# Attention and gated FFN on one core: when the first weights, the second quarters' scores, the output weights and batch 1's turns are issued

## The chip, the cores and the metric

One core of a Trainium2 chip runs the whole kernel. The time of a run is the device time in microseconds (us) of that core. The engines are TensorE (PE in the profile; PEld is its weight load), VectorE (DVE), ScalarE (ACT), GpSimd (POOL) and SyncE (SP, which here only issues DMAs). Each has its own queue of instructions and works through it in order; an instruction that waits holds up all that stand behind it on its engine. DMAs are issued from two queues: SyncE's (q1 in the profile) and GpSimd's (q0).

## The reference: what is computed

Attention over 8 batches of 8 heads, 576 positions, head size 64, with 16 beacon keys and values in front that every query sees; then a feed-forward network over the 4,608 rows that result.

```
k_all, v_all = concat(beacon_k, k), concat(beacon_v, v)      # 592 keys
scores = q @ k_all.T / sqrt(D)                               # causal, except for the beacons
a = softmax(scores)
x = (a @ v_all) with the heads side by side                  # 4608 x 512
out = (relu(x @ w_gate) * (x @ w_val)) @ w_out               # d_ff 1536
```

Inputs and output are float32; the kernel computes in bf16 with float32 sums.

## The kernel before, in words

**Attention.** Scores are made transposed, keys on the partitions and queries along the row, so exp's result is at once the moving operand of the product with v. A *unit* (L319) is one slot of up to 1,024 scores per partition: `qk` (L329) writes it into one of two double-bank PSUM buffers (`s_ps`), `exp` (L340) is one ScalarE instruction over it, and where the causal diagonal crosses it GpSimd sets the upper part to zero (the mask, L351). A part of a unit is named (g, ci, kt): g is the half of the heads (0 for heads 0 to 3, 1 for heads 4 to 7), ci the chunk of queries (240, 256 and 80 of them), kt the tile of 128 keys. When all parts of a chunk are through exp, the next step runs `av` (L363; its matmuls stand at L379): the product with v and, with a column of ones, the row sums. Then VectorE takes the reciprocal of the sums (`invert`, L387) and scales into xT (`scale`, L392). `note` (L396) keeps the least and greatest reciprocal in two VectorE operations, for a test at the end of the program whether a general path is needed; it has no other use.

**FFN.** A tile of 512 rows of x gives twelve `up` groups (four matmuls with wg at L413, ReLU on ScalarE at L416, four matmuls with wv at L422, the product hT on VectorE at L424) and then four `down` groups (twelve matmuls with wo at L429, a ScalarE copy at L432, a store). The products of `up` lie in two FFN banks (`f_ps`), or the second of them in an `s_ps` buffer where `spare` is set.

**The order of work.** The program is written out step by step in one Python loop over `plan` (L463), and each engine keeps that order. Batch 0 has steps 0 to 6, two units a step. Steps 7 to 10 have no attention, only FFN work of batch 0: no group, three, three, two. Batch 1 has steps 11 to 17 with one FFN group each; from step 18 on, seven steps a batch with FFN groups by a credit of time. `s2` in the code is 11, batch 1's first step. Within a step the order is: the `qk` of both units (with `between[s]` after the first), exp of the first unit, `av` and `invert` of the chunks that are due, the first half of the planned loads and casts, the FFN groups with exp of the second unit and `scale` among them, the rest of the planned actions, and then `later_half[s]`, what `after(s, ...)` registered.

**How data comes in.** Batches 0 and 1 bring q and k in *quarters*: 256 positions (i = 0 or 1) of four heads (g), cast to bf16 and turned on TensorE by eight transposes (L282), then moved from PSUM into qT or kT (L283). Batch 0's quarters are loaded by SyncE and cast by an engine (`cast_first`), batch 1's are loaded and cast by GpSimd's DMA (`load_second`, L271). Their last 64 positions (*tails*) and the beacon keys are turned by `turn_rows` (L300). Later batches bring tiles of 128 rows by SyncE, three loads a step, cast them on GpSimd a step later (L245, L249) and turn q and k with a DMA transpose another step later (L254); `fetch` (L584) registers this, and batch 2's starts in step 10. Batch 1's five value tiles are loaded by SyncE after a one-element memset on GpSimd (L227) lets the first go; casts of the values stand on GpSimd.

**The weights.** `load_w` (L309) issues two casting DMAs from GpSimd for a range of columns of wg or wv, `load_wo` (L315) one for half of wo. Before the change: columns 0 to 383 of both in `after(0)`, behind the casts of batch 0's first two value tiles; the rest of wg in `after(1)`, of wv in `after(2)`; wo in `after(7)`, behind batch 1's quarter loads.

The diff touches the order of the units (L140), the helpers from L498 to L520, the registrations up to L582 and the loop from L621 to L665.

Of the kernel before, what the change touches and what calls it, by code (L numbers as in the profile page):

```python
# [16 lines left out]
def general_path(tc, q, k, v, beacon_k, beacon_v, out, ident, wg, wv, wo):  # L17
# [123 lines left out]
    ((0, 0, 0),), ((0, 0, 1), (1, 0, 1)), ((1, 0, 0),), ((0, 1, 3), (1, 1, 3)),  # L141
    ((0, 1, 2),), ((0, 1, 1),), ((0, 1, 0),), ((1, 1, 2),), ((1, 1, 1),), ((1, 1, 0),),
# [11 lines left out]
def kernel(  # L154
# [15 lines left out]
    P = 128  # L170
# [298 lines left out]
    with tc.manual_schedule():  # L469
# [25 lines left out]
        def f_quarter():  # L495
            return f_ps.tile([P, 2, 2, P], BF16, name="f")

        def turn_first(i, g):  # L498
            first.turn_quarter("k", i, g, f_quarter(), dve)()
            first.turn_quarter("q", i, g, f_quarter(), act if i == 0 and g == 0 else dve)()  # L500

        def cast_first(i, g):
            first.cast_quarter("k", i, g, dve)
            first.cast_quarter("q", i, g, act if i == 0 else dve)
# [5 lines left out]
        def load_both(n0, n1):  # L510
            load_w(wg, moe_w_gate, n0, n1)
            load_w(wv, moe_w_val, n0, n1)

        def turn_two(x, i):
            for n in "kq":
                ps = s_ps.tile([P, 2, NP, 2, P], BF16, name="s")
                for move in [x.turn_quarter(n, i, g, ps[:, g, :2], (dve, act)[g])
                             for g in range(2)]:
                    move()
# [8 lines left out]
        later_half, between = {}, {}  # L528

        def after(step, action):  # L530
            later_half.setdefault(step, []).append(action)
# [5 lines left out]
        def turn_second_half():  # L537
            for g in range(2):
                turn_first(1, g)

        between[0] = lambda: turn_first(0, 1)
        after(0, lambda: cast_first(1, 0))
# [3 lines left out]
        after(0, lambda: load_both(0, 384))  # L546
        between[1] = turn_second_half
# [6 lines left out]
        after(3, lambda: turn_tails(first))  # L554
# [10 lines left out]
        after(7, lambda: load_wo(0, 6))  # L565
        after(7, lambda: load_wo(6, 12))
        for t in range(NKT):
            after(s2 - 1 + t // 2, lambda t=t: second.cast("v", t, pool))

# [10 lines left out]
        after(s2 - 1, lambda: turn_two(second, 0))  # L580
        after(s2, lambda: turn_two(second, 1))
# [25 lines left out]
        for s, (b, i, quota) in enumerate(plan):  # L607
# [14 lines left out]
            for j, u in enumerate(units):  # L622
                u.qk()
                if j == 0 and s in between:
                    between[s]()
            if units:
                units[0].exp()
            chunks, due = due, []
# [17 lines left out]
            for j, (kind, _, run) in enumerate(mine):  # L646
                if j == 0 and other and (kind == "down" or len(mine) == 1):
                    other.pop().exp()
                ups = kinds.count("up")
                run(b is None or (ups > 1 and j == (1 if ups > 2 else 0)))  # L650
                if j == 0:
                    for c in chunks:
                        c.scale()
                        notes.append(c.note)
                if other:
                    other.pop().exp()
            if not mine:
                for c in chunks:
                    c.scale()
                    notes.append(c.note)  # L660
                if other:
                    other.pop().exp()
            for act_ in acts + later_half.pop(s, []):
                act_()
            while len(notes) > (6 if s < 8 else 3 if s == 8 else 0):  # L665
                notes.pop(0)()
# [8 lines left out]
        run_sp()  # L675
        for t0, _ in spans:
            queue += ffn_tiles[t0 // M_TILE].groups(0, M_TILE, 0, M_TILE // P)
# [42 lines left out]
```

## Time and profile before

| | us |
|---|---|
| five runs | 398.41, 399.14, 398.06, 397.07, 399.34 |
| their median | 398.41 |
| the profiled execution, its own time | 399.94 |
| its span, first to last instruction | 398.2 |
| TensorE busy | 371.7 (93%) |
| VectorE, ScalarE, GpSimd busy | 207.3, 191.2, 121.3 |
| first `up` matmul, first `down` matmul | 32.88, 72.85 |
| mean granted TensorE clock | 0.992 |
| moved by DMA | 49.84 MB |

A group line of the profile names the line of the kernel, the engine, the operation, the tile written and the one read, the count, and the busy time with the mean of one instruction in ns; behind the last bar stands the idle time of that engine just before, and what ended it. In the timeline the first number is the start from the span's first instruction, the second the length. In the chain of work that ended last, each line is a piece of time and who held the work up in it. A table of stretches gives busy us of each engine between two moments, the granted TensorE clock as a share of full speed, the busy share of the DMA engines and what they moved. The DMA view counts packets, bytes and time for each queue.

### The profile page before, as it was taken

The numbers are of one execution on the slowest core, as the hardware profiler recorded it, in microseconds if no ns is written. First come the engines' busy times: TensorE is split into PE (matmuls) and PEld (weight loads), VectorE is DVE, ScalarE is ACT, GpSimd is POOL, SyncE is SP. The second block draws the span as 40 slices with busy tenths as digits, with TensorE's granted clock in tenths as the row PEclk, the third lists the DMA queues.
The fourth block names the chain that finished last, engine by engine and source line by source line (L and its number), as shares of the span: only waits on it lengthen the run. The fifth ranks groups of instructions, "written<-read, shape, count | busy, mean of one in ns | idle before, by whom it ended". The sixth has DMA issues, their size and how long they took to land.

```text
span 398.2 us, 10157 instructions
## 1 busy us (share of the span) xinstructions
PE 371.7 (93%) x4265; PEld 187.2 (47%) x4265; DVE 207.3 (52%) x336; ACT 191.2 (48%) x264; POOL 121.3 (30%) x213
## 2 busy tenths in 40 slices
PE   3778858999999999999999999999999999999994
PEld 2454433554554455545454545444544454444441
DVE  3766727736663666455646574557455643512420
ACT  3562264556463655465546455645455633323321
POOL 1858039424342335233524351435111100000000
PEclk9999998999999999999999999999999999999998
DMA  7999997949934882488348933985200011011002
GB/s 214 203 207 191 175 239 164 180 141 213 184 80 128 204 181 61 134 203 186 74 113 197 207 78 101 208 194 92 96 28 2 2 57 50 2 48 59 2 28 85
DMA packets 145555, 49.84 MB, mean 125 GB/s; under 512 B 133216, under 2 KB 139872, under 8 KB 145504
## 3 DMA queue, kind: packets, MB, share of 16 engines
q1 hardware_dynamic: 137536, 43.37, 46.4%
q0 software_dynamic: 7968, 5.77, 9.8%
q8 instruction: 35, 0.57, 0.6%
q14 instruction: 16, 0.13, 0.1%
HBM read 38.27 MB, written 9.44 MB: 120 GB/s over the span
## 4 chain that ended last, share of the span: by engine, by line
PE 88%; DVE 5%; DMA 2%; POOL 2%; issue 1%; ACT 1%; SPq 0%; DVEq 0%; POOLq 0%; ACTq 0%
PE f L413 24%; PE f L429 24%; PE s L422 12%; PE f L422 11%; PE ab L379 7%; PE s L335 6%; PE os L379 3%; DVE r L387 2%; DMA wide<-in_q_dram 1%; DVE hT L424 1%; DMA raw<-in_v_dram 1%; DVE xT L392 1%; POOL e L351 1%; DVE least L399 0%; POOL v L245 0%
## 5 line engine op out<-in xcount | busy, mean ns | idle before, releaser
L343 ACT ACTIVATE e<-s 128x1024 bf16<-128x1024 f32 (+2 forms) x112 | 105.0, 962 | 29.8 <-PE s L335 29.2
L413 PE MATMUL f<-xT,wg 128*128 128x512 bf16 x432 | 112.0, 382 | 0.8 <-DVE r L387 0.8
L416 ACT ACTIVATE g<-f 128x512 f32<-128x512 f32 x108 | 64.6, 598 | 88.9 <-PE f L413 84.7
L351 POOL TENSOR_SCALAR_AFFINE_SELECT e<-e 128x512 bf16<-128x512 bf16 (+2 forms) x80 | 46.5, 592 | 169.5 <-ACT e L343 158.8
L429 PE MATMUL f<-wo,hT 128*128 128x512 bf16 x432 | 97.3, 379 | 0.0
L387 DVE RECIPROCAL r<-os 128x240 f32<-128x240 f32 (+2 forms) x45 | 61.0, 1355 | 55.4 <-PE os L379 54.8
L424 DVE TENSOR_TENSOR hT<-g,s 128x512 bf16<-128x512 f32 x56 | 38.4, 687 | 60.5 <-PE s L422 59.5
L422 PEld LDWEIGHTS <-wv 128*128 128x128 bf16 x432 | 42.4, 98 | 53.0 <-issue 3.0
L429 PEld LDWEIGHTS <-hT 128*128 128x128 bf16 x432 | 41.0, 98 | 48.5
L424 DVE TENSOR_TENSOR hT<-g,f 128x512 bf16<-128x512 f32 x52 | 35.7, 687 | 51.4 <-PE f L422 50.7
L413 PEld LDWEIGHTS <-wg 128*128 128x128 bf16 x432 | 39.4, 98 | 46.6 <-issue 1.5
L422 PE MATMUL s<-xT,wv 128*128 128x512 bf16 x224 | 57.5, 379 | 0.3 <-DVE hT L424 0.3
L432 ACT COPY ob<-f 128x512 f32<-128x512 f32 x36 | 21.1, 586 | 74.2 <-PE f L429 54.9
L422 PE MATMUL f<-xT,wv 128*128 128x512 bf16 x208 | 54.2, 384 | 0.3 <-DVE hT L424 0.3
L379 PE MATMUL ab<-e,v 128*32 128x80 bf16 (+4 forms) x1320 | 40.2, 236 | 5.1 <-POOL e L351 3.1
L249 POOL CAST half<-raw 128x512 bf16<-128x512 f32 (+2 forms) x60 | 36.4, 624 | 15.3 <-DMA raw<-in_k_dram 6.3
L335 PE MATMUL s<-qT,kT 64*128 64x80 bf16 (+3 forms) x704 | 36.3, 237 | 4.0 <-DVE qT L283 1.7
L335 PEld LDWEIGHTS <-kT 64*128 64x128 bf16 x704 | 21.4, 98 | 27.4 <-issue 25.0
L379 PEld LDWEIGHTS <-v 128*32 128x32 bf16 (+1 forms) x1408 | 27.2, 99 | 14.0 <-issue 8.2
L379 PE MATMUL os<-e,ones 128*32 128x240 bf16 (+4 forms) x660 | 32.6, 234 | 0.0
L245 POOL CAST v<-raw 128x512 bf16<-128x512 f32 (+1 forms) x40 | 25.9, 653 | 14.1 <-DMA raw<-in_v_dram 14.1
L392 DVE TENSOR_TENSOR xT<-ab,r 128x480 bf16<-128x480 f32 (+2 forms) x45 | 24.9, 553 | 0.7
(47 smaller groups left out, 123.0 us busy)
## 6 DMA issues: line engine op xcount, KB each, us to landing
out_dram<-ob SPq DMA_DIRECT2D x36, 256.0 KB, 2.1
raw<-in_v_dram SPq DMA_DIRECT2D x24, 256.0 KB, 4.8
raw<-in_q_dram SPq DMA_DIRECT2D x24, 256.0 KB, 4.1
raw<-in_k_dram SPq DMA_DIRECT2D x18, 256.0 KB, 3.7
raw<-in_v_dram SPq DMA_DIRECT2D x8, 224.0 KB, 3.4
wo<-in_moe_w_out_dram POOLq DMA_DIRECT2D x2, 768.0 KB, 12.2
raw<-in_k_dram SPq DMA_DIRECT2D x6, 224.0 KB, 3.3
raw<-in_v_dram SPq DMA_DIRECT2D x8, 160.0 KB, 3.7
```

Source lines behind the costliest of these rows:

```text
L249: copy(h[:n], raw[:n])
L335: nc.tensor.matmul(self.s[:, a, c + j * n:c + (j + 1) * n], self.batch.kT[rows, 2 * g + j, kt * P:(kt + 1) * P], self.batch.qT[rows, 2 * g ...
L343: nc.scalar.activation(e[:, :k * 4 * n].rearrange("p (k a x) -> p a k x", k=k, a=2), self.s[:, :, :k * 2 * n].rearrange("p a (k x) -> p a ...
L351: nc.gpsimd.affine_select(out=cols[:, :, :m], in_=cols[:, :, :m], pattern=[[0, 4], [1, m]], compare_op=ALU.is_ge, fill=0.0, base=base, cha ...
L379: nc.tensor.matmul(o[:, q0 - cq0:q0 - cq0 + n], w, e[:kr, 2 * (hh % 2) + hh // 2], start=(i == 0 and part != 1), stop=(i == self.last), sk ...
L387: nc.vector.reciprocal(self.r[:, :n], self.os[:, :n])
L392: nc.vector.tensor_mul(xT[:, 2 * self.g:2 * self.g + 2, t0:t0 + n], self.ab[:, :, :n], self.r[:, :n].unsqueeze(1).to_broadcast([P, 2, n]))
L413: nc.tensor.matmul(g[:, :n], wg[:, ki, nf * P:(nf + 1) * P], x[:, ki], start=(ki == 0), stop=(ki == KM - 1))
L416: nc.scalar.activation(gs[:, :n], g[:, :n], AF.Relu)
L422: nc.tensor.matmul(u[:, :n], wv[:, ki, nf * P:(nf + 1) * P], x[:, ki], start=(ki == 0), stop=(ki == KM - 1))
L424: nc.vector.tensor_mul(self.h[:, nf, c0:c1], gs[:, :n], u[:, :n])
L429: nc.tensor.matmul(o, self.h[:, nf, ms * P:(ms + 1) * P], wo[:, nf, :], start=(nf == 0), stop=(nf == NF - 1))
```

## The change

Five edits of the order, with no change in what is computed.

- Columns 0 to 383 of wg and wv are issued by GpSimd right after the first q quarter has been moved into qT: a copy of one element from qT to wg makes GpSimd wait for that move. They no longer stand in `after(0)`.
- In the units of batches 0 and 1, (0, 1, 2), of heads 0 to 3, comes ahead of the pair (0, 1, 3), (1, 1, 3). In step 1 the exp of the first unit comes ahead of the turns; the second quarters of heads 0 to 3 are turned between the two `qk`s, those of heads 4 to 7 behind them (`behind`). The move and the cast of one q quarter pass from VectorE to ScalarE, and one pair of casts comes earlier in step 0 (`mid`). Batch 0's tails are turned in step 4 behind its `qk`s, not at the end of step 3.
- wo's two DMAs move from `after(7)` to the end of step 10, behind the casts of batch 1's first two value tiles.
- Batch 1's quarters are turned in FFN banks: the first half after the first `up` of step 10, the second half in step 11 behind its `qk`s and ahead of its `up`; before, both were turned in `s_ps` buffers at the ends of these steps.
- Notes: in steps 7 to 10 one is taken after each FFN group; from step 11 on two are kept back, and what is left is taken after the loop.

```
--- before.py
+++ after.py
@@ -138,8 +138,8 @@
 
 
 UNITS_BY_CHUNK = (
-    ((0, 0, 0),), ((0, 0, 1), (1, 0, 1)), ((1, 0, 0),), ((0, 1, 3), (1, 1, 3)),
-    ((0, 1, 2),), ((0, 1, 1),), ((0, 1, 0),), ((1, 1, 2),), ((1, 1, 1),), ((1, 1, 0),),
+    ((0, 0, 0),), ((0, 0, 1), (1, 0, 1)), ((1, 0, 0),), ((0, 1, 2),),
+    ((0, 1, 3), (1, 1, 3)), ((0, 1, 1),), ((0, 1, 0),), ((1, 1, 2),), ((1, 1, 1),), ((1, 1, 0),),
     ((0, 2, 4), (0, 2, 3), (0, 2, 2)), ((0, 2, 1), (0, 2, 0)),
     ((1, 2, 4), (1, 2, 3), (1, 2, 2)), ((1, 2, 1), (1, 2, 0)),
 )
@@ -497,24 +497,24 @@
 
         def turn_first(i, g):
             first.turn_quarter("k", i, g, f_quarter(), dve)()
-            first.turn_quarter("q", i, g, f_quarter(), act if i == 0 and g == 0 else dve)()
+            first.turn_quarter("q", i, g, f_quarter(), act if g == 0 else dve)()
 
         def cast_first(i, g):
             first.cast_quarter("k", i, g, dve)
-            first.cast_quarter("q", i, g, act if i == 0 else dve)
+            first.cast_quarter("q", i, g, dve if (i, g) == (1, 1) else act)
 
         cast_first(0, 0)
         turn_first(0, 0)
         cast_first(0, 1)
 
-        def load_both(n0, n1):
-            load_w(wg, moe_w_gate, n0, n1)
-            load_w(wv, moe_w_val, n0, n1)
+        nc.gpsimd.tensor_copy(wg[:1, 0, :1], first.qT[:1, 0, :1])
+        load_w(wg, moe_w_gate, 0, 384)
+        load_w(wv, moe_w_val, 0, 384)
 
         def turn_two(x, i):
             for n in "kq":
-                ps = s_ps.tile([P, 2, NP, 2, P], BF16, name="s")
-                for move in [x.turn_quarter(n, i, g, ps[:, g, :2], (dve, act)[g])
+                ps = f_ps.tile([P, NP, 2, P], BF16, name="f")
+                for move in [x.turn_quarter(n, i, g, ps[:, 2 * g:2 * g + 2], (dve, act)[g])
                              for g in range(2)]:
                     move()
 
@@ -525,7 +525,7 @@
             x.turn_rows(x.tails[0], x.kT[:, :, 528:592], dve)
             x.turn_rows(x.tails[1], x.qT[:, :, 512:576], dve)
 
-        later_half, between = {}, {}
+        later_half, between, behind, mid = {}, {}, {}, {}
 
         def after(step, action):
             later_half.setdefault(step, []).append(action)
@@ -534,24 +534,21 @@
         second.beacon = second.load_rows(beacon_k[1])
         load_tails(second)
         s2 = BASE[1]
-        def turn_second_half():
-            for g in range(2):
-                turn_first(1, g)
 
         between[0] = lambda: turn_first(0, 1)
-        after(0, lambda: cast_first(1, 0))
+        mid[0] = lambda: cast_first(1, 0)
         after(0, lambda: cast_first(1, 1))
         after(0, lambda: first.cast("v", 0, pool))
         after(0, lambda: first.cast("v", 1, pool))
-        after(0, lambda: load_both(0, 384))
-        between[1] = turn_second_half
+        between[1] = lambda: turn_first(1, 0)
+        behind[1] = lambda: turn_first(1, 1)
         after(1, lambda: load_w(wg, moe_w_gate, 384, 1536))
         after(2, lambda: first.cast("v", 2, pool))
         after(2, lambda: first.cast("v", 3, pool))
         after(2, lambda: load_w(wv, moe_w_val, 384, 1536))
         after(2, lambda: cast_tails(first, dve))
         after(3, lambda: first.cast("v", 4, pool))
-        after(3, lambda: turn_tails(first))
+        behind[4] = lambda: turn_tails(first)
 
         def load_second(i):
             for g in range(2):
@@ -562,10 +559,10 @@
         after(7, lambda: load_second(1))
         for t in range(NKT):
             after(7, lambda t=t: second.load("v", t, t == 0))
-        after(7, lambda: load_wo(0, 6))
-        after(7, lambda: load_wo(6, 12))
         for t in range(NKT):
             after(s2 - 1 + t // 2, lambda t=t: second.cast("v", t, pool))
+        after(s2 - 1, lambda: load_wo(0, 6))
+        after(s2 - 1, lambda: load_wo(6, 12))
 
         def cast_small(x):
             x.beacon = x.cast_rows(x.beacon, dve)
@@ -577,8 +574,8 @@
 
         after(s2 - 3, lambda: cast_small(second))
         after(s2 - 2, lambda: turn_small(second))
-        after(s2 - 1, lambda: turn_two(second, 0))
-        after(s2, lambda: turn_two(second, 1))
+        mid[s2 - 1] = lambda: turn_two(second, 0)
+        behind[s2] = lambda: turn_two(second, 1)
         after(s2 + 1, wide_ctx.close)
 
         def fetch(b, s0):
@@ -621,10 +618,17 @@
                 units = [Unit(batches[b], order[2 * i + x]) for x in range(2)]
             for j, u in enumerate(units):
                 u.qk()
-                if j == 0 and s in between:
-                    between[s]()
-            if units:
+                if j == 0:
+                    if s == 1:
+                        u.exp()
+                    if s in between:
+                        between[s]()
+            if units and s != 1:
                 units[0].exp()
+            if units and s in mid:
+                mid[s]()
+            if s in behind:
+                behind[s]()
             chunks, due = due, []
             for c in chunks:
                 c.av()
@@ -652,8 +656,12 @@
                     for c in chunks:
                         c.scale()
                         notes.append(c.note)
+                    if b is None and s in mid:
+                        mid[s]()
                 if other:
                     other.pop().exp()
+                if b is None and notes:
+                    notes.pop(0)()
             if not mine:
                 for c in chunks:
                     c.scale()
@@ -662,7 +670,7 @@
                     other.pop().exp()
             for act_ in acts + later_half.pop(s, []):
                 act_()
-            while len(notes) > (6 if s < 8 else 3 if s == 8 else 0):
+            while len(notes) > (6 if s < s2 else 2):
                 notes.pop(0)()
             for u in units:
                 for g, ci, _, _ in u.parts:
@@ -673,6 +681,8 @@
                         if not done:
                             ready[s + 2] = b * S + CHUNKS[ci][0] + CHUNKS[ci][1]
         run_sp()
+        for note in notes:
+            note()
         for t0, _ in spans:
             queue += ffn_tiles[t0 // M_TILE].groups(0, M_TILE, 0, M_TILE // P)
         for j, (_, _, run) in enumerate(queue):
```

## Prediction

> **What bounds the kernel now.** I read the busy shares by slice first, then a table of stretches, then the chain of work, then the DMA view of short stretches. All times are us of the profiled execution; x.x stands for the moment on its clock.
>
> ```profile
> PE   3778858999999999999999999999999999999994
> PEclk9999998999999999999999999999999999999998
> ```
>
> ```profile
> 50.00:60.40 10.40, 4.95 (x81) 2.88 (x77) 2.61 (x5) 6.51 (x9) 3.71 (x8) 1.00 1.10 239
> 60.40:72.80 12.40, 11.14 (x133) 5.17 (x133) 9.19 (x11) 6.95 (x9) 9.27 (x16) 0.86 0.84 183
> 72.80:398.00 325.20, 319.89 (x3525) 158.13 (x3521) 163.41 (x260) 157.11 (x221) 84.21 (x148) 1.00 0.46 108
> ```
>
> The columns are length, PE, PEld, DVE, ACT, POOL busy, clock, DMA share, GB/s. From 72.8 on, TensorE is full, and the list of its waits for that stretch is empty. So the change can be worth only what it moves the first `down` (L429, begun at 72.85), as long as batch 2 is there when TensorE comes for it. Ahead of 72.85, two places are loose: 10 to 33 (first `up` at 32.88) and 50 to 64.3. The second, in the chain:
>
> ```profile
> 53.86 0.69 DVE hT L424
> 54.54 0.61 DVE kT L283
> 55.20 3.83 DMA raw<-in_v_dram
> ...
> 59.17 0.63 POOL v L245
> 59.80 0.60 POOL e L351
> ...
> 60.44 0.30 PE ab L379 x8
> ```
>
> GpSimd runs in order. In step 11 it has the mask of unit 0, the casts of batch 2's first k, q, v, and only then the masks of unit 1, which batch 1's first `av` needs. The v of batch 2 landed at 59.1. So TensorE stands until 60.44, and then pays again:
>
> ```profile
> 57.46:60.87 3.41, 0.43 (x13) 0.29 (x13) 0.03 (x1) 1.16 (x2) 2.26 (x4) 1.00 1.14 258
> 60.87:64.28 3.41, 3.41 (x10) 1.01 (x10) 1.62 (x1) 0.60 (x1) 3.41 (x7) 0.50 0.51 93
> ```
>
> Why was that load late? SyncE's rings were full of batch 1's values (issues from 37.81 for 14.99 us), and these crawled beside wo:
>
> ```profile
> q0 software_dynamic: 621, 0.62, 91.6%
> q1 hardware_dynamic: 617, 0.15, 29.7%
> ```
>
> That is 45 to 49: q0 (GpSimd's) moves wo in packets of 1,024 bytes, q1 (SyncE's) rows of 256 bytes. As many packets each, so four times the bytes for wo. Alone, q1 made 3,592 packets in 53 to 57, some 900 per us against 154.
>
> In the first stretch GpSimd is the link:
>
> ```profile
> 13.20 1.21 POOL L245 CAST v<-raw 128x512 bf16<-128x512 f32 x2
> 14.36 1.54 POOL L311 DMA_DIRECT2D wg<-in_moe_w_gate_dram  x2
> 15.89 1.42 POOL L311 DMA_DIRECT2D wv<-in_moe_w_val_dram  x2
> 17.33 1.75 POOL L351 TENSOR_SCALAR_AFFINE_SELECT e<-e 128x448 bf16<-128x448 bf16 x3
> ```
>
> The mask of unit 2 waits behind four weight issues (its exp ended near 12.8), and `av` of chunk (1,0) waits for it until 17.97.
>
> **What the skill says.** The Trainium skill, DMA: Bandwidth & Descriptors, Queues, rings and completion order: an SDMA engine takes turns between its queues packet by packet. The trace agrees (621 to 617). TensorE: Matmul & The Clock Gate, Part 1: after about 3.4 us of idleness the array runs at half clock for such a window. It agrees: 0.43 us busy in 3.41, then a window at 0.50. SBUF — State Buffer, Who interferes with whom: a VectorE operation with two SBUF inputs can be shut out by GpSimd. It agrees: the `least` note at 65.48 beside a busy GpSimd took 2.06, their median is 0.40.
>
> **Part 1, first weights issued early.** Removed at 14.36: 1.54 + 1.42 = 2.96 us of GpSimd. Added: a copy of one element that waits for the first qT move (ScalarE, 6.30 to 6.89), then the same four issues, some 7.15 to 10.1. The copy has no row; the one-element memset took 0.09, I bound it by 0.05 and 0.3 and take 0.1. Queued behind it on GpSimd is the mask of unit 0, which began at 9.96: at most 0.2 late, covered until unit 1. So the issue itself is a gain. Its transfer is not. The first q0 packet followed its issue by 1.77 (14.36 to 16.13); here 8.9. The four make 1,024 packets of 768 bytes, at some 170 per us (17 to 18 shows 189 and 174 for the two queues) busy until 14.9. What is still to come on q1 at 9.0, in issue order: the last q quarter (512 packets), beacon v (128), v0 (896), v1 to v2, both tails, v3 (1,024 each pair or tile), v4. Before, they ran at 238 GB/s (8 to 16): v0 through by about 11.2, v1 by 12.3. Now the first 1,000 packets go at 165: the last q quarter at 12.2 for 10.0, v0 at 15.75, v1 16.9: 4.5 late. Landing is seen some 1.5 after such a count.
> So: VectorE's cast of the last q quarter, waiting to about 13.7, holds the kT move behind it; QK of unit 3 goes at 15.1, not at 14.7. GpSimd's v1 cast ends near 19.1; `av` (0,0) ends near 19.6 for 16.1. Bound: 16 (q1 not held up) to 21.
>
> **Part 2, heads 0-3 first, exp of unit 2 ahead of the turns, moves and casts shared with ScalarE, tails turned in step 4.** Unit (0,1,2) needs only one pair of second quarters. Priced alone it would save about 1 us before `av` (0,0) and the idle 2.07 of ScalarE at 23.67 (tails turned before QK). But `av` (0,1) still follows, on VectorE, from the end of `av` (0,0): two reciprocals and two scalings (1.66 + 0.66, twice), tail casts 1.36, turn 0.3: 6.3 with handovers. Before it took 7.9 (16.08 to 23.98), since `av` (1,0) waited for the mask. 19.6 + 6.4 = 26.0 for 23.98. From the end of `av` (0,1) to the first `up` the chain is VectorE's four reciprocals and scalings, 6.57 (26.31 to 32.88), unchanged. First `up`: 34.9, **+2.0**; bounds 31.6 and 36.7.
>
> **Part 3, fill.** Notes one per `up` in steps 8 to 10 (0.8 each, in a cadence of 1.73 per `up` beside an hT of 0.69: hidden): the 0.65 wait at 42.2 goes. Turns of batch 1 in the f banks, between `up`s and ahead of step 11's `up`: the same 64 transposes, 4 times 0.65, but the moves of 0.69 and 0.59 lie under an `up`; ahead of 50.9 and 55.8 they stood open. Counted: eight `up`s 13.9, tails 1.15, turns 2.6, QKs 1.6, ninth `up` 1.75, bank waits 0.5: TensorE comes to the second half of `av` (0,0) of batch 1 21.5 after the first `up`, 56.4. Before: 60.44, 27.6 after.
>
> **Part 4, wo behind the values.** The gate of v0 (a memset after the eight hwide issues) comes 2.63 before + 6.15 after the first `up`'s time, at 38.5; q1's packets from 40.4, alone, 920 per us. v1 is through at 42.6, cast by 45; then wo's two issues (1.65), first packet near 46.75. Through v0 of batch 2 q1 has 7,808 packets; 5,840 are gone by then, 1,968 are left beside wo's 1,536. wo takes 10.2 us as before (41 to 51 there), so both end near 57. The cast of batch 2's v is again what stands ahead of the mask: landing 58.6, cast 0.63, mask 0.60: `av` at **59.9**, only 0.5 before today's 60.44. TensorE, there at 56.4, stands again, for 3 us instead of nothing. wo itself is due at the first `down`, 69.7: covered by 11 us.
>
> **Part 5, from there to the first `down`.** Before 12.06 (60.79 to 72.85). One `up` at half clock cost 3.5 for 1.73: 1.7 goes if the window stays busy enough (stretch 53.8 to 57.5, 2.17 of 3.66 busy, kept the clock). Notes kept back by two chunks free VectorE of 2.4 in step 12, of which 0.75 was on the path. 9.6 remains: **−2.45**. The two notes left over run beside the last FFN tile: nothing.
>
> **Sum.** −0.5 − 2.45 = −2.95. The profiled execution took 399.94 (span 398.2 and 1.7 around it), 1.5 above the median of 398.41. So 397.0 for it, and **395.5** as a median. Batch 2: its k and q of tile 3 were turned by about 79.6, TensorE came at 83.9; its chain on SyncE (turn of k0 at 58.91, then 5.2 a step) starts 0.6 to 1.2 earlier, so up to 4.9 us fit before it binds.
>
> **Rivals.** (a) *The window goes cold again.* Idle for 3 of 3.4 us, as before; it depends on where the window lies. Then 1.7 of part 5 is lost: 397.2. (b) *The values aren't starved.* If q1 keeps its pace at 9 to 15, the first `up` comes at 31.6, everything behind it 3.3 earlier: −6.2, 392.2. For it: DMA shares before showed gaps at 10 to 15; against it: 189 to 174. (c) *Slower: v3 falls behind the big weight load.* wg's columns 384 to 1536 are issued once GpSimd is past v1's cast and two masks, first packet near 22.2; v3 is through at 20.2. q0 makes about 96 of those packets per us (575 in 24 to 30), so q1 does too: 300 packets of v3 caught cost 3 us in `av` (0,1). That moves the first `up` to 38 or 39 and the mask of step 11 past 63: +2, 400.5. It decides from 2 us of slip. (d) *Nothing*: the stall only moves from wo-before-values to wo-before-batch-2 with a cold window and a slow front; it lies between (a) and (c), near 398.3.
>
> **Chances.** Forecast 0.42 (394 to 397), (a) 0.18, (b) 0.18, (d) 0.1, (c) 0.12. Below 0.3% (1.2 us) nothing can be told from no change. (a) is split at that line, so faster 0.65, same 0.2, slower 0.15. Range: from (b), a little under, to between (d) and (c): 391.5 to 400.
>
> **What would show it.** The v0 and v1 casts of batch 0 near 17.5 and 18.5 instead of 13.2; first `up` near 35; batch 1's values cast soon after landing, near 44; q0 and q1 at equal packets from 47 to 57; GpSimd waiting for v of batch 2 near 58; one window's clock. The forecast is wrong if the first `up` is before 32.9, if step 11's masks don't wait for a load, or if TensorE waits in step 18.

## The result, and the profile after

| | before | after |
|---|---|---|
| median, us | 398.99 (79 runs) | 400.58 (42 runs) |
| after / before, 95% interval | | 1.0035 [1.0023, 1.0046] |
| profiled execution: own time, span | 399.94, 398.2 | 402.56, 400.9 |
| first `up`, first `down` matmul | 32.88, 72.79 | 32.89, 75.32 |

The change makes the kernel slower by 0.35%, where 395.5 was forecast. Each profile is one execution, and the profiled ones of before and after took 0.95 and 1.98 us more than these medians, those of e2, e8 and e9 3.1, 3.3 and 4.7 more than theirs and that of e3 2.6 less, so a microsecond or two between two profiles proves nothing by itself. Moments are the starts of instructions in the timeline; the 72.85 that stood for the first `down` before is a piece of the chain, which begins 0.06 later.

The busy shares of the profile after, and its table of stretches (columns as before: length, PE, PEld, DVE, ACT, POOL busy, clock, DMA share, GB/s):

```profile
PE   3778866999999999999999999999999999999994
...
PEclk9966996999999999999999999999999999999998
```

```profile
53.00:63.17 10.17, 4.26 (x70) 2.54 (x69) 2.36 (x4) 5.39 (x7) 3.02 (x6) 0.87 1.04 193
63.17:75.32 12.15, 11.31 (x137) 5.40 (x136) 6.51 (x7) 6.88 (x9) 8.96 (x16) 0.82 0.82 180
75.32:400.90 325.58, 319.89 (x3528) 158.14 (x3521) 163.66 (x264) 157.07 (x221) 85.61 (x148) 1.00 0.45 108
```

TensorE's work after the first `down` is the same 319.89 us as before, in a stretch of 325.58 for 325.20. The end stands as far behind the first `down` as it did; the whole loss was there by 75.32. Of the 2.5 us at the first `down` some 1.0 is the longer execution that was profiled after the change: by the medians the loss is 1.6. The stall of step 11 is still where it was, and longer. In the chain of work:

```profile
46.72 14.67 DMA raw<-in_v_dram
...
61.90 0.63 POOL v L245
62.53 0.60 POOL e L351
...
63.17 0.40 PE ab L379 x8
```

Before, the same links read 59.17, 59.80 and 60.44: batch 2's first v, cast; the mask behind that cast; the second half of `av` (0,0) of batch 1 behind the mask. All are now 2.7 later. The timeline of GpSimd says what the time went on; in brackets is the idle time before an instruction and what ended it:

```profile
43.08 2.16 POOL L245 CAST v<-raw 128x512 bf16<-128x512 f32 x2 [5.74 <-DMA raw<-in_v_dram]
45.18 1.65 POOL L316 DMA_DIRECT2D wo<-in_moe_w_out_dram  x2
...
57.90 0.61 POOL L249 CAST half<-raw 128x512 bf16<-128x512 f32 x1 [2.78 <-DMA raw<-in_q_dram]
61.90 0.63 POOL L245 CAST v<-raw 128x512 bf16<-128x512 f32 x1 [3.38 <-DMA raw<-in_v_dram]
62.48 1.22 POOL L351 TENSOR_SCALAR_AFFINE_SELECT e<-e 128x512 bf16<-128x512 bf16 x2
```

Batch 1's values are cast 6 us earlier than before (43.08 for 49.43), as the change meant. wo, issued behind them at 45.18, has packets from 47.17 to 60.5 (before 39.6 to 52.1), and batch 2's k, q and v crawl beside it in place of batch 1's values. The DMA view of 50 to 54:

```profile
q0 software_dynamic: 608, 0.61, 92.5%
q1 hardware_dynamic: 583, 0.15, 28.0%
```

These are the shares that the prediction showed for 45 to 49 of the kernel before (621 and 617 packets), moved five us down the clock. At the front, GpSimd's timeline has the early weights, and a new wait:

```profile
7.43 0.18 POOL L510 COPY wg<-qT 1x1 bf16<-1x1 bf16 x1 [5.88 <-ACT qT L283]
7.91 1.55 POOL L311 DMA_DIRECT2D wg<-in_moe_w_gate_dram  x2 [0.31 <-POOL wg L510]
...
12.97 1.20 POOL L245 CAST v<-raw 128x512 bf16<-128x512 f32 x2
...
29.64 0.62 POOL L245 CAST v<-raw 80x512 bf16<-80x512 f32 x1 [6.27 <-DMA raw<-in_v_dram]
30.22 0.90 POOL L351 TENSOR_SCALAR_AFFINE_SELECT e<-e 128x320 bf16<-128x320 bf16 x2
```

v0 and v1 of batch 0 came in time (12.97), `av` (0,1) began at 21.14 for 23.98; then v4's cast waited for its load until 29.64, while the big weight loads filled the other queue (packets from 18.25 to 32.67), the last masks stood behind that cast, and the first `up` came at 32.89. A front that was 2.8 us ahead had lost all of it by then.

### The profile page after: what moved, and what is told of

It is laid out like the page before. It is cut to its first block, busy times and chain, and to the rows that moved or that the text cites. A ratio compares the mean times of both kernels' runs of the same rounds, so it can differ in the third digit from the quotient of the medians.

```text
span 400.9 us, 10156 instructions
## 1 busy us (share of the span) xinstructions
PE 373.5 (93%) x4265; PEld 188.2 (47%) x4265; DVE 203.3 (51%) x334; ACT 192.0 (48%) x266; POOL 123.3 (31%) x214
## 4 chain that ended last, share of the span: by engine, by line
PE 86%; DMA 7%; issue 2%; SPq 2%; POOL 1%; DVE 1%; ACT 0%; POOLq 0%; DVEq 0%; ACTq 0%
PE f L413 24%; PE f L429 24%; PE s L422 12%; PE f L422 11%; PE ab L379 6%; PE s L335 6%; DMA raw<-in_v_dram 6%; PE os L379 3%; DMA wide<-in_q_dram 1%; SPq L230 1%; SPq L290 1%; POOL e L351 0%; DVE hT L424 0%; POOL wv L311 0%; POOL v L245 0%
## 5 line engine op out<-in xcount | busy, mean ns | idle before, releaser
L422 PE MATMUL s<-xT,wv 128*128 128x512 bf16 x224 | 58.4, 383 | 0.0
L249 POOL CAST half<-raw 128x512 bf16<-128x512 f32 (+2 forms) x60 | 36.8, 633 | 12.2 <-issue 5.5
L245 POOL CAST v<-raw 128x512 bf16<-128x512 f32 (+1 forms) x40 | 27.4, 691 | 17.2 <-DMA raw<-in_v_dram 17.2
```

The source lines that it names most:

```text
L245: copy(self.v[:n, t].rearrange("p (h a d) -> p h a d", a=2, d=C), raw[:n].rearrange("p (h d a) -> p h a d", a=2, d=C))
L249: copy(h[:n], raw[:n])
L422: nc.tensor.matmul(u[:, :n], wv[:, ki, nf * P:(nf + 1) * P], x[:, ki], start=(ki == 0), stop=(ki == KM - 1))
```

## The experiments

The edits are to the kernel after unless "before" is named; ratios are to runs of the kernel before that were made beside them (medians 399.27 to 399.57), with 95% intervals, so the medians of two rows are not compared. The theories of the expectations: **S**, GpSimd's casts wait for loads that GpSimd's own transfers have slowed, and masks stand behind those casts; **T**, the loss is TensorE's waits for the turns in FFN banks, and its half clock; **M**, what counts is that masks stand behind casts of loads; **Z**, the DMA engines are full up to batch 2's first tiles, so batch 2 comes when all that is ahead of it has been moved; **N**, the loss is in the new order of units and turns. The moments of all profiled executions are collected here; "MB" is what both queues had moved when GpSimd began the cast of batch 2's first v. In e5, e6, e7, e12 and e15 (marked *) that cast stands at the end of step 12 and waits for no load; there the value had landed at 59.80, 58.66, 60.91, 60.95 and 59.90.

| kernel | median, us | ratio | first `up` | batch 2's v0 | MB | first `down` |
|---|---|---|---|---|---|---|
| before | | 1 | 32.88 | 59.17 | 12.00 | 72.79 |
| after | 400.58 | 1.0035 | 32.89 | 61.90 | 12.15 | 75.32 |
| e1 | 400.08 | 1.0020 | 32.14 | 61.25 | 12.17 | 74.83 |
| e2 | 401.37 | 1.0029 | 33.06 | 63.45 | 12.18 | 76.88 |
| e3 | 404.76 | 1.0140 | 32.26 | 53.13 | 10.62 | 66.39 |
| e4 | 402.65 | 1.0091 | 31.53 | 61.17 | 12.16 | 74.59 |
| e5 | 400.47 | 1.0008 | 34.26 | 65.39* | 12.74 | 68.26 |
| e6 | 398.18 | 0.9965 | 32.48 | 64.63* | 12.81 | 67.04 |
| e7 | 401.55 | 1.0055 | 33.39 | 65.37* | 12.72 | 69.07 |
| e8 | 401.19 | 1.0027 | 35.35 | 63.28 | 12.07 | 76.93 |
| e9 | 400.58 | 1.0025 | 35.14 | 63.24 | 12.17 | 78.00 |
| e10 | 399.65 | 0.9995 | 32.38 | 59.25 | 11.96 | 72.67 |
| e11 | 399.26 | 0.9999 | 31.38 | 57.89 | 12.05 | 71.31 |
| e12 | 401.67 | 1.0045 | 32.65 | 64.73* | 12.72 | 67.42 |
| e13 | 398.87 | 1.0002 | 32.84 | 58.35 | 12.01 | 69.92 |
| e14 | 400.19 | 1.0020 | 31.32 | 59.97 | 12.05 | 72.80 |
| e15 | 398.88 | 1.0000 | 31.25 | 64.05* | 12.73 | 66.47 |
| e16 | 396.98 | 0.9939 | 33.46 | 54.33 | 10.62 | 67.47 |

**One part undone, one step moved (e1 to e4).** e1 puts the first weights back behind batch 0's first two casts; e2 puts wo back into step 7.

```
-        nc.gpsimd.tensor_copy(wg[:1, 0, :1], first.qT[:1, 0, :1])
-        load_w(wg, moe_w_gate, 0, 384)
-        load_w(wv, moe_w_val, 0, 384)
...
         after(0, lambda: first.cast("v", 1, pool))
+        after(0, lambda: load_w(wg, moe_w_gate, 0, 384))
+        after(0, lambda: load_w(wv, moe_w_val, 0, 384))
```

> The changed kernel with part 1 alone undone: the first weight columns go back behind the casts of batch 0's first two value tiles. Theory S (two casts on GpSimd wait for loads that GpSimd's own weight transfers delay, v4 of batch 0 at 29.64 and v of batch 2 at 61.90): the big wg load starts some 3 us later, v4 is through before it, its cast waits less than 1 us, first up near 31.5 instead of 32.89, but wo still stands before batch 2's v: 399 +- 1. Theory T (the turns in FFN banks, two waits of 1.0 for ScalarE's kT move, and the half clock in front of the fill are the loss; the late loads are covered): no gain, 400.6 or later.

```
+        after(7, lambda: load_wo(0, 6))
+        after(7, lambda: load_wo(6, 12))
...
-        after(s2 - 1, lambda: load_wo(0, 6))
-        after(s2 - 1, lambda: load_wo(6, 12))
```

> The changed kernel with part 4 alone undone: wo again ahead of batch 1's values. Theory S: the wait moves back from batch 2's v to batch 1's values, the mask of step 11 near 60.5 instead of 62.5, one half-clock window instead of two: 398 +- 1, first up unchanged at 32.9. Theory T: wo's place is no matter, 400.6.

e1: 1.0020 [1.0003, 1.0037], e2: 1.0029 [1.0003, 1.0055]. Neither is the whole cause, and neither can be told from the change itself. e3 issues wo in step 11, behind the casts of batch 2's first k, q and v:

```
             for act_ in acts[:len(acts) // 2]:
                 act_()
+            if s == s2:
+                load_wo(0, 6)
+                load_wo(6, 12)
```

> The changed kernel with wo issued later still, in step 11 behind the casts of batch 2's first k, q, v (ahead of unit 1's masks). Theory S: batch 2's v is cast near 50, GpSimd is free when unit 1's exp ends, the second half of av (0,0) comes at 59 instead of 63.2 with the full clock; wo lands near 62, before the first down: 395 +- 1.5. If the first down has to wait for wo, less. Theory T: 400, since turns and front are as before.

1.0140 [1.0107, 1.0172], where S had 395. The stall of step 11 went, as S had it, and the first `down` came at 66.39. But the next tiles of batch 2 now ran beside wo, and a mask of step 14 stood behind their casts. TensorE's timeline:

```profile
76.69 0.62 PE L379 MATMUL ab<-e,v 128*32 128x256 bf16 x8 [6.15 <-POOL e L351]
```

e4 issues the big weight loads behind batch 0's casts, so that v4 is not held up:

```
-        after(1, lambda: load_w(wg, moe_w_gate, 384, 1536))
...
         after(2, lambda: first.cast("v", 3, pool))
-        after(2, lambda: load_w(wv, moe_w_val, 384, 1536))
+        after(2, lambda: load_w(wg, moe_w_gate, 384, 1536))
...
         after(3, lambda: first.cast("v", 4, pool))
+        after(3, lambda: load_w(wv, moe_w_val, 384, 1536))
```

> The changed kernel with the big weight loads behind the values: wg's columns 384 to 1536 in step 2 behind the casts of v2 and v3, wv's in step 3 behind v4's. Theory S: v4's cast is done by 21, no wait of 1.75 in the last av of group 0, first up near 30.3, then the rest 2.5 earlier: 398 +- 1, unless the fourth up (near 35) waits for wv. Theory T: first up is set by VectorE's chain alone and stays near 32.9; 400.6.

1.0091 [1.0059, 1.0124]. v4 was cast at 23.16 for 29.64 and the first `up` came 1.4 earlier, at 31.53, yet batch 2's v0 moved by 0.7 only, and the time rose. Why it rose is not shown: the profile is of the fastest of its six runs. S is right at these places and wrong on what they are worth: a wait that was taken away came back at a later load. That led to Z.

**The masks ahead of the casts (e5, e6, e7, e12).** In step 11, batch 2's casts move behind the masks of unit 1, the v0 cast to the end of step 12. e5 does so in the kernel after, e6 in the kernel before; e7 is e5 with e4.

```
+            if s == s2:
+                after(s2 + 1, acts.pop(2))
+            first_half = 0 if s == s2 else len(acts) // 2
...
-            for act_ in acts[:len(acts) // 2]:
+            for act_ in acts[:first_half]:
```

> The changed kernel; only GpSimd's order in step 11 differs: unit 1's masks stand ahead of the casts of batch 2's first k and q, and the cast of its first v moves to the end of step 12. No DMA is issued earlier. Theory M (the cost is a mask that stands behind casts of loads; what is late is not needed yet): second half of av (0,0) near 59 instead of 63.2, full clock after it, first down near 70; then the mask of step 14, still behind the casts of batch 2's k3 and q3 (74 to 75.5), takes some 3 of it back: 397.5 +- 1.5. Theory Z (the transfers up to batch 2's tiles are one full sum, whatever the order, and step 18 waits for them): TensorE only waits elsewhere, 400 +- 1.

> The same edit of step 11 in the kernel before. Theory M: second half of av (0,0) near 57.5 instead of 60.4, no half-clock window, then the mask of step 14 (73.1) takes back part: 397 +- 1.2 where the kernel before has 399.3. Theory Z: 399.3 +- 0.8.

> The changed kernel with both the edit of step 11 and the big weight loads behind batch 0's values (first up at 31.5 in that kernel). Theory M: av (0,0) near 56, 1 less than the edit of step 11 alone as far as step 14's mask allows: 397 +- 1.5. Theory Z: 400 or, with the fill ended sooner and the same transfers to wait for, 401.

e5 1.0008 [0.9985, 1.0030], e6 0.9965 [0.9943, 0.9988], e7 1.0055 [1.0033, 1.0078]. In all three the stall of step 11 is gone and the first `down` comes at 67 to 69, 5.5 to 7.1 us earlier than without the edit; most of that is given back behind it, for a large part in step 14. In e6 (the kernel before):

```profile
72.48 0.61 POOL L249 CAST half<-raw 128x512 bf16<-128x512 f32 x1 [4.04 <-issue]
73.38 0.61 POOL L249 CAST half<-raw 128x512 bf16<-128x512 f32 x1 [0.28 <-DMA raw<-in_q_dram]
73.94 0.63 POOL L351 TENSOR_SCALAR_AFFINE_SELECT e<-e 128x512 bf16<-128x512 bf16 x1
```

```profile
74.63 0.40 PE L379 MATMUL ab<-e,v 128*32 128x256 bf16 x8 [3.59 <-POOL e L351]
```

e6 is faster than both kernels, the one version that computes the result and is. For e5 the quotient of the medians is 1.0031, at the edge of its interval, so its place between the two kernels stays open. e12 carries the idea on to steps 11 to 17, in the kernel before:

```
+            first_half = 0 if s2 <= s < s2 + STEPS else len(acts) // 2
```

> The kernel before with masks ahead of the casts of loads in steps 11 to 17, not in step 11 alone: batch 2's loads, casts and turns of these steps all stand in their second half. Theory M (masks behind casts are what TensorE waits for): the wait of 3.59 us in step 14 that the narrower edit left goes, 397.0 within 0.5. Theory Z (the chain of batch 2 is late by itself): the wait turns up at step 18's first QK or at the turns' k0, 398.2 within 0.5. If the casts that come later now hold their staging tiles, and so the next loads, longer: 399 or more.

1.0045 [1.0023, 1.0066]: slower. The wait for a mask of step 14 went, and a longer one stood at `av` of batch 1's last chunk, whose masks came behind the casts of batch 2's last tiles:

```profile
78.89 0.61 POOL L249 CAST half<-raw 80x512 bf16<-80x512 f32 x1 [2.56 <-issue]
80.24 0.61 POOL L249 CAST half<-raw 64x512 bf16<-64x512 f32 x1 [0.74 <-DMA raw<-in_q_dram]
81.23 0.63 POOL L245 CAST v<-raw 80x512 bf16<-80x512 f32 x1 [0.39 <-DMA raw<-in_v_dram]
81.81 0.90 POOL L351 TENSOR_SCALAR_AFFINE_SELECT e<-e 128x320 bf16<-128x320 bf16 x2
```

```profile
82.34 0.33 PE L379 MATMUL ab<-e,v 80*32 80x80 bf16 x8 [6.24 <-POOL e L351]
```

Masks stay behind whatever was cast in the step before, and the next loads start later: batch 2's second, third and fourth v are issued at 58.54, 64.98 and 71.02, in e6 at 57.95, 63.98 and 70.48. M falls as a general rule.

**The turns (e8, e13).** e8 puts batch 1's turns back into score buffers; e13 does that part of the change alone, in the kernel before.

```
-                ps = f_ps.tile([P, NP, 2, P], BF16, name="f")
-                for move in [x.turn_quarter(n, i, g, ps[:, 2 * g:2 * g + 2], (dve, act)[g])
+                ps = s_ps.tile([P, 2, NP, 2, P], BF16, name="s")
+                for move in [x.turn_quarter(n, i, g, ps[:, g, :2], (dve, act)[g])
...
-        mid[s2 - 1] = lambda: turn_two(second, 0)
-        behind[s2] = lambda: turn_two(second, 1)
+        after(s2 - 1, lambda: turn_two(second, 0))
+        after(s2, lambda: turn_two(second, 1))
```

> The changed kernel with the turns of batch 1 back in the score banks at the ends of steps 10 and 11. Theory T (the two waits of 1.05 and 0.96 for ScalarE's kT move cost time): some 1.5 less, 399. Theories M and Z: TensorE only comes sooner or later to the same wait for the mask (62.5), 400.6 +- 0.8, with the idle time ahead of the second half of av (0,0) changed and its moment the same.

> The kernel before with one part of the change alone: the turns of batch 1's quarters go through the FFN's PSUM banks, in step 10 behind the first up and in step 11 behind the exp. If these turns are the rest of the loss: 400.0 or more where the kernel before has 399.2, with waits of about 1 us of the ups for the moves of kT, and no gain at step 11. If what sets the end is batch 2's loads (theory Z): 399.2 within 0.4, v0's cast within 1 us of 59.2.

e8 1.0027 [1.0000, 1.0054], e13 1.0002 [0.9979, 1.0025]. The turns do make `up`s wait, 1.05 and 0.96 us in e13 as in the kernel after, but ahead of a stall that takes such waits up: T falls as far as the turns go. Its other half, the half clock, is taken up under Part 5 below.

**One part alone (e9, e10, e11, e14).** e9 and e10 are e1's and e2's edits turned round and made in the kernel before: the early weights alone, the late wo alone. e11 is the kernel after with weights, wo, turns and notes put back, so the new order alone; e14 is e11 with wo in step 10.

> The kernel before with one part of the change alone: the first 384 columns of wg and wv are issued ahead of step 0, once the first q is turned. Theory Z (the DMA engines are full up to batch 2's tiles, and the step that sets the end is batch 2's chain of casts and turns): av(0,0) starts about 1 us earlier, the first up moves by less than 1 us (the change without this part has it 0.75 earlier), time 399.3 to 399.9 where the kernel before has 399.2. Theory N (the loss comes from the new order of units and turns, not from transfers): 399.2 within 0.4. If early weights are a gain by themselves, under 398.6.

> The kernel before with one part of the change alone: wo is issued in step 10, behind the casts of batch 1's first values. Theory Z: wo's packets then run beside batch 2's k0, q0 and v0, v0's cast comes 2 to 3 us later than 59.2, and the first down and the turns of batch 2 with it: 400.3 to 401.3, most of the loss of the change. Theory N: 399.2 within 0.4, since with wo back in step 7 the change stayed as slow. The prediction's own Part 4 would give 398.7.

> The change with the first weights, wo, the turns of batch 1 and the notes put back: what is left of it is heads 0-3 of the second quarters first, their casts and moves shared with ScalarE, and the tails turned in step 4. Theory N: 400.3 to 401, the loss of the change in this part alone; the first up at 32 and v0's cast at 60.5 or later. Theory Z with wo at fault: 399.0 to 399.5, v0's cast within 0.5 of 59.2. The prediction's Part 2 (2.0 us to the worse with starved values) had no gain here either.

> The new order of units with wo in step 10, and the weights, the turns and the notes as before. If the late wo costs only where the values are asked for earlier: 400.0 or more, v0's cast at 60.5 or later where the new order alone had it at 57.9. If not, 399.2 within 0.4, v0's cast at 57.5 to 58.5, and the rest lies with the turns and the notes.

e9 1.0025 [1.0006, 1.0044], e10 0.9995 [0.9977, 1.0013], e11 0.9999 [0.9981, 1.0017], e14 1.0020 [1.0004, 1.0036]. So the early weights lose by themselves; on which path they do isn't shown, since e9's profile is one of the long ones. N falls: the new order alone loses nothing. Its front gains (first `up` 31.25 to 32.14 in e1, e11, e14 and e15, against 32.38 to 32.88 in before, e6, e10, e12 and e13), without a gain in the time that can be told. The late wo alone changes nothing that can be told either, against both forecasts for it: Z had batch 2's v0 2 to 3 us later, and it was cast at 59.25 for 59.17; Part 4 of the prediction had a gain, 398.7. With wo behind the values the new order loses 0.2%, as e1 does, which is e14 with the FFN-bank turns and the new notes; these two add nothing that can be told. The difference between e11 and e14, and that between before and e10, are each uncertain by some 0.25%, so how much of the 0.2% is the late wo alone is not settled.

**The best front with the masks ahead, and no wo (e15, e16).** e15 is e11 with e6's edit. e16 is the kernel after with wo's transfer left out.

> The new order alone, with masks ahead of batch 2's casts in step 11 (the edit that made the kernel before 0.35% faster). If the front's gain (first up 1.2 earlier in the run of the new order alone) reaches batch 2's chain: 397.3 within 0.6, faster than both kernels. If the chain ignores it: 398.2 within 0.4, as the edit alone gave.

```
+    nc.vector.memset(wo, 0.0)
...
-        nc.gpsimd.dma_start(wo[:, i0:i1],
-                            moe_w_out.rearrange("(ko ki) n -> ki ko n", ki=P)[:, i0:i1])
+        nc.gpsimd.memset(wo[:1, i0:i1, :1], 0.0)
```

> The change with wo's transfer left out: wo is set to 0 once at the start by VectorE, and each issue is replaced by a GpSimd memset of one row (the downs then multiply with zeros). Theory Z (DMA engines full up to batch 2's tiles): 1.57 MB less to move, at some 150 GB/s about 10 us, so v0's cast at 50 to 54 for 61.9, no wait in step 11, turn k0 near 53, and 394 to 397. Theory T (TensorE's own waits and clock): the waits for turns stay and the time is 399 to 401.

e15 1.0000 [0.9980, 1.0021], outside both forecasts: the gains of e6 and of the front don't add. e16 0.9939 [0.9913, 0.9965], by the ratios 1.0% below the kernel after. GpSimd in e16, where L245 and L249 have become L246 and L250:

```profile
53.22 1.16 POOL L250 CAST half<-raw 128x512 bf16<-128x512 f32 x2
54.33 0.63 POOL L246 CAST v<-raw 128x512 bf16<-128x512 f32 x1
56.05 1.22 POOL L351 TENSOR_SCALAR_AFFINE_SELECT e<-e 128x512 bf16<-128x512 bf16 x2 [1.09 <-ACT e L343]
```

No cast waits for a load, and the masks now follow exp. The step 11 stall has gone with nothing reordered.

**What they say together.** In the eleven kernels that cast batch 2's v0 ahead of the masks with wo's transfer before it (before, after, e1, e2, e4, e8 to e11, e13, e14), the cast began when 11.96 to 12.18 MB had been moved, be it at 57.9 or at 63.5. In e3 and e16, which hadn't moved wo by then, it was 10.62 MB, and 10.62 + 1.57 is 12.19. Much of this follows from the order of the loads, since what stands ahead of v0 on SyncE's queue is the same everywhere. What the runs add is that wo was through before the cast as well, wherever it was issued. So Z holds for what must be moved and not for the moment, which spread over 5.6 us at the same count: the pace decides that.

The pace of the kernel after was lower in two places. It was 2 us ahead at 5 MB (22.3 for 24.2), level at 8 MB (39.5 in both), and 1 us behind at 12 MB (60.2 for 59.2); landing, seen after the count, came later as well. First, between 26 and 34 its q0 moved some 160 GB/s for 206 before, since the early weights were through and the quarter loads of batch 1, behind v4's cast on GpSimd, began no sooner than before (31.07 for 30.28). Second, the way from 10 to 12 MB took 9.5 us for 8.3. It took 8.3 to 9.2 in six profiles with wo ahead of the values (before, e6, e11, e12, e13, e15) and 9.3 to 10.8 in eight with wo behind them (after, e1, e4, e5, e7, e8, e10, e14), but also 10.2 and 10.0 in the long ones of e2 and e9, which have wo ahead. That the late wo lowers the pace is likely, then, and not shown.

The loss has two shares that experiments show, the early weights (0.25%, e9) and the late wo with the new order (0.2%, e14). Their intervals are as wide as the shares, and the way from either of them to the end is argued from single profiles.

## Why the prediction was wrong, step by step

**What bounds the kernel: right.** The end is the first `down` plus a constant: from it to the last store's issue it was 320.6 in before, after and e1, e2, e4, e8 to e11 and e14 (321.7 in e13, 321.2 in e16). Where the stall of step 11 goes, it is no longer constant (326.0 in e6, 329.3 in e3, 329.0 in e12): batch 2's loads bind behind. The "4.9 us of slack" of batch 2 held for its turns, not for the masks of steps 14 to 16, which the step didn't price.

**Part 1, early weights: right on the mechanism, mis-sized, and on one tile too few.** It had the casts of v0 and v1 near 17.5 and 18.5 and the first packet at 8.9. The copy came at 7.43, so the packet came at 10.5 and the mask of unit 0 at 11.26, 1.3 later than before where at most 0.2 was allowed. In the kernel after, v0 and v1 were in time. But the same front gave in e5

```profile
14.41 0.63 POOL L245 CAST v<-raw 128x512 bf16<-128x512 f32 x1 [1.74 <-DMA raw<-in_v_dram]
17.43 0.63 POOL L245 CAST v<-raw 128x512 bf16<-128x512 f32 x1 [2.39 <-DMA raw<-in_v_dram]
```

and v1 at 15.95 in e3 and 16.03 in e8. Which value pays differs from one execution to the next: v4 was cast at 29.64, 23.96, 25.03 and 32.10 in after, e3, e5 and e8. That v4 can fall behind the big load is rival (c)'s mechanism, one tile later than it was placed.

**Part 2: right alone, and left out of the sum.** The new order was priced at about 1 us alone and, beside starved values, not credited in the first `up`. Means of the first `up` over single profiles: 32.65 with the old order (before, e6, e10, e12, e13), 31.5 with the new one and late weights (e1, e11, e14, e15), 33.7 with the new one and early weights (after, e3, e5, e8, which lie between 32.26 and 35.35). So the order gave about 1.1 and the early weights cost about 2.2: +1.0 where +2.0 was forecast. In the profile after itself it was 0.0.

**Part 3, fill: too short.** TensorE was to reach the stalled half of `av` 21.5 after the first `up`; it took 25.8 (58.65). The bank waits put at 0.5 were 0.85, 1.05, 0.53 and 0.96, and the first `up`s ran at half clock, 1.87 for 1.03. This cost nothing: the stall took it up.

**Part 4 is the step that failed**: "wo takes 10.2 us as before (41 to 51 there), so both end near 57". That is wo at its full pace; the trace of before has its packets from 39.6 to 52.1, 12.5 us, and over all runs they took 10.9 to 13.9. After the change they took 13.4: 70 in each of the first two us, then 136 to 155, and a tail to 60.5. Batch 2's v0 was to be counted through 10.25 after wo's first packet. It took 11.7 (47.17 to 58.84), with 2,246 packets of q1 left where 1,968 were forecast; in e1, e4, e10 and e14 it took 11.2 to 11.9. The landing was seen 2.55 after the count and not 1.6 (0.99 in before), and the cast began 0.5 behind the landing. So the landing came at 61.4 for 58.6 and `av` at 63.17 for 59.9: 2.7 later than before, where 0.5 earlier was forecast. Behind the mis-sized term stands a thought that was missing. The step moved wo from the values to batch 2 and asked how the queues share there; it did not count what must have been moved by the moment that the mask waits for, which is nearly the same in both kernels (12.00 and 12.15 MB). e10 makes the same move in the kernel before: v0 was counted through at 56.91, near the 57 of the forecast, but landed 2.19 later, and `av` came at 60.52 for 60.44.

**Part 5 failed with it.** From the stalled half of `av` to the first `down` it took 12.35 us before and 12.15 after, so 0.2 of the 2.45 came. The stall was 4.52 and not 3, and the clock went down, rival (a)'s mechanism:

```profile
57.19:60.60 3.41, 1.46 (x23) 0.64 (x22) 0.69 (x1) 2.47 (x4) 0.61 (x1) 1.00 1.19 241
60.60:64.02 3.42, 0.85 (x14) 0.38 (x14) 0.29 (x1) 0.00 (x0) 2.12 (x4) 0.50 0.48 109
64.02:67.43 3.41, 3.41 (x15) 1.20 (x14) 1.48 (x2) 0.60 (x1) 3.41 (x7) 0.50 0.53 103
```

That a warm clock there is worth what was said is seen in e13, whose stall was 2.96:

```profile
59.62:69.92 10.30, 9.33 (x132) 4.86 (x132) 8.82 (x11) 6.88 (x9) 8.48 (x14) 1.00 0.83 175
```

10.30 for the 12.35 of before, with TensorE busy 9.33 for 11.19 on 132 and 133 matmuls; the notes, the other term of Part 5, are as before there. Whether a stall lets the clock go down depended on where it lay, as rival (a) said. The clock of these traces changes in steps of 3.41 us. Counted from the change at 27.58, e13's stall lies across two of them, which kept 1.78 and 2.09 us of work, and the clock stayed full; e8's was shorter, 2.66, but left its step 1.19, and the half clock followed. In the kernel after, steps with 1.46 and 0.85 were each followed by half clock.

**The sum.** `av` came 3.27 later than forecast and Part 5 gave 2.25 less: 5.5 us at the first `down`, 75.32 for 69.8. In the medians it is 4.5 (+1.6 for −2.95), as the execution profiled after the change was a longer one than that before. The 395.5 also started from 398.41, the median of five runs, which 79 runs put at 398.99.

**The rivals.** (b), values not starved, came true at v0 and v1 of the profile after and was worth nothing there, since v4 took it back. (d), "the stall only moves from wo-before-values to wo-before-batch-2 with a cold window and a slow front", describes the trace best, and was priced too low, at no loss, by the same 10.2. (c)'s time, 400.5, was met on another path, and so by luck: its first `up` at 38 or 39 never came.

## What to carry to other kernels

Where the DMA engines are full, find the moment that the stalled instruction really waits for and count the bytes that must be moved by then. The count says what can't be avoided; the moment depends on the pace as well, here by up to 5.6 us at one count. An edit that leaves the count alone can gain at that wait only by raising the pace, however many waits it takes away on the way, or by putting the work that waits ahead of the load, as e6 did. And when a stall is removed, price the next instruction of the same kind: here each mask that came free was followed, some steps on, by one behind a later cast.

## What the runs showed of the hardware that was not expected

- A transfer's end has a tail: of wo's 1,536 packets in the kernel after, 1,464 were begun by 58.0 and the last ended at 60.5; v0's landing, which needs all its packets, was seen 2.55 after its packets were counted through. Over all runs this lag was 0.6 to 3.2 us, and no one order of the transfers explains it: it was 0.94 to 0.99 in before, e11 and e13, 1.57 to 2.55 in the six kernels after, e1, e4, e8, e10 and e14 with wo behind the values, but 1.9 to 3.2 in e2, e9, e12 and e15, which have wo ahead.
- Identical instructions up to 33 us left v1's cast anywhere from 13.5 to 17.4 and v4's from 24.0 to 32.1 (after, e3, e5, e8). e5 and e8, run on one chip, had v4 at 25.0 and 32.1. How two crowded queues share differs from one execution to the next, and one profile of it is one draw.
